# Recurrent state with an MLP behind it: one operand transposed once, kept in DRAM, and a gap between two preparation steps

## The chip, the cores and the metric

The kernel runs on one core of a Trainium2 chip. A core has a matrix engine (PE, whose weight loads are listed as PEld), a vector engine (DVE), a scalar engine (ACT), a general engine (POOL, also called GpSimd) and SyncE (SP), which here does nothing but issue DMAs. Each engine works through its own list of instructions in the order in which the program wrote them, and waits on semaphores for the others. DMAs of one core share 16 transfer engines. The metric is the device time of one execution in microseconds (us); the time of a kernel is the median of its runs.

## The reference

Six inputs r, k, v, w, a, b have the shape (4, 8, 768, 40): 4 batches, 8 heads, 768 tokens and 40 numbers per token. For each of the 32 heads a 40x40 state runs along the tokens; each token first reads the state, then changes it. The outputs of all heads of a token form a row of 320 numbers, which goes through two matrices with a piecewise quadratic gate between them.

```python
for t in range(S):
    y[:, :, t] = np.einsum('bhd,bhde->bhe', rt, state)
    Sa = np.einsum('bhde,bhe->bhd', state, at)
    state_decay = state * wt[:, :, None, :] - np.einsum('bhd,bhe->bhde', Sa, bt)
    state = state_decay + np.einsum('bhd,bhe->bhde', vt, kt)
...
x = np.ascontiguousarray(attn_out.transpose(0, 2, 1, 3)).reshape(B * S, H * D)
h = x @ w_in
g = np.where(pos, h, np.where(neg, 0.0, (h + beta) ** 2 / (4.0 * beta)))
return (g @ w_out).astype(np.float32)
```

w_in is 320 x 2048, w_out 2048 x 320, all in float32.

## The kernel before

**Chunks, halves and sets.** The 768 tokens are cut into 24 chunks of 32 tokens, and four chunks make a set of 128 tokens, of which there are six (numbered 0 to 5). Inside a chunk the recurrence is written as matrix products; only the state passes from chunk to chunk. Each chunk is worked on in two halves, `hb` 0 and 1, of 16 heads each. The heads of a half stand in two groups of partitions, 0 to 63 and 64 to 127 (`f` is 0 or 1).

**Three preparation steps, set by set.** They run ahead of the chunks that use them.

- *Token rows* (`prelude`, lines 232 to 278). In four parts of eight tokens: running products of w with two scans on DVE (line 221), then R, V and the scaled K, P, A and B. P is w's running product, A and B are a and b multiplied or divided by it. The results are gathered in the tile `arena` and stored by POOL to the DRAM buffer `scr` (line 275), which has one row of 240 numbers per head and token: R, V, K, P, A, B, 40 each. R and V are copied from DRAM to DRAM by `copy_rv` (line 129). Every part begins with POOL clearing two columns of `wz` (line 246) and ACT copying w into it (line 247).
- *Pair products* (`ab_set`, lines 292 to 324). For each of the set's four chunks, A and B of all 32 heads are loaded into the tile `tiab` (`load_rows`, line 290, four DMAs), transposed by DVE into `ea` (line 304) half by half, and multiplied on PE (line 313) to 32x32 products of each pair of tokens. ACT copies them to `pairs` (line 320). There is one `tiab`; the next chunk's load waits until the transposes have read it.
- *Inverse* (`invert`, lines 326 to 351). A triangular solve of 31 steps, each with two instructions on POOL (lines 343 and 349). `adopt` (line 357) takes the result over when the set's first chunk begins.

Sets 0 and 1 are prepared at the start by functions of their own: `early_products`, then `early_turn` (line 187 transposes A and B by PE, ACT copies them out in line 189 to `turned`), `early_ab` (line 203) and `early_store` (line 211). The tiles of `turned` are borrowed from the cg buffers and from `Y`; `init_cg` clears the cg buffers afterwards.

**A chunk.** For each half, `load_ti` (line 414) loads R, V, K, P and A of 16 heads into `tih`, with four DMAs, and `load_cg` loads V, K and B into one of three `cg` buffers, with four DMAs (lines 423 and 426). `turn` transposes on DVE: part 0 A into cg (line 442, two instructions), part 1 V and K into `ev`, part 2 R and P into `pr` (line 447). `scores` multiplies them on PE (line 457) and masks the products into cg (line 466). `chain` has four steps, each ending in a yield: lines 488 to 492, 498 to 509, 511 to 545, and 551 to 560.

**The MLP.** Per 64 tokens, `relayout` moves Y into X with nine DMAs (lines 574, 580, 584), and `moe` issues the first product (line 603), the gate (lines 611 to 613), a split into two floats (ACT line 619, POOL line 620) and the second product (line 632). Its matmuls are fed between the steps of the chunks by `fill`.

**What sets the order.** The order of each engine's list is written out by hand, at the end of the function: a chunk has four stages, each with one step of each half's chain, the turns, scores and loads of the next chunk, and a `fill`. `fill` calls `background` six times, which advances the three preparation steps. `WINDOWS` says for the sets 1 to 5 from when to when, in tenths of a chunk, a step is spread out; each step is a generator that yields weights (`ROWS_W`, `AB_W`, `INV_W`), and `background` advances it until the sum of its weights is the share of the window that has passed. A window of (0, 0) stands for the work done at the start. All loads of a chunk, all loads of the preparation, `copy_rv`, the relayout and the output go through the one list of SP, in this order of writing.

```python
WINDOWS = dict(
    rows=[(0, 0), (14, 36), (38, 62), (66, 102), (106, 142)],
    ab=[(0, 0), (36, 44), (62, 79), (102, 119), (142, 159)],
    inv=[(12, 38), (44, 78), (81, 118), (121, 158), (161, 198)],
)
```

Of the kernel before, what the change touches and what calls it, by code (L numbers as in the profile page):

```python
# [24 lines left out]


WINDOWS = dict(
    rows=[(0, 0), (14, 36), (38, 62), (66, 102), (106, 142)],
    ab=[(0, 0), (36, 44), (62, 79), (102, 119), (142, 159)],
    inv=[(12, 38), (44, 78), (81, 118), (121, 158), (161, 198)],  # L30
)

SHARE = (1.4, 0.6) * 2
SLOTS = len(SHARE)

ROWS_W = (2, 2, 4, 2, 6, 6, 4)
AB_W = (1, 4, 1, 4, 12, 15)
INV_W = 12

# [11 lines left out]
def rwkv_moe_kernel(ctx: ExitStack, tc: tile.TileContext, r, k, v, w, a, b, w_in, w_out, ident_d, mask_d, out):  # L51
# [28 lines left out]
    wz = const.tile([128, D, 10], F32, name="wz")  # L80
    dz = const.tile([128, D, 10], F32, name="dz")
    tiab = const.tile([128, 16, 80], F32, name="tiab")
    tih = [const.tile([128, 8, 200], F32, name=f"ti{i}") for i in range(2)]
    lw = const.tile([128, 2048 + 256], F32, name="lw")
    cgf = [const.tile([128, 16 * CW + 24], F32, name=f"cg{i}") for i in range(3)]
    cgs = [x[:, 0 : 16 * CW].rearrange("p (h x) -> p h x", x=CW) for x in cgf]
# [8 lines left out]
    work = ctx.enter_context(tc.tile_pool(name="work", bufs=1))  # L95
    scr = [dram.tile([NH * 128 + 1, RW], F32, name=f"scr{s}") for s in range(NS)]
    scr4 = [x[0 : NH * 128].rearrange("(b c t) x -> c b t x", c=4, t=L) for x in scr]
    pairs = const.tile([128, 32, 32], F32, name="pairs")
    tinv = const.tile([128, 4, 8, 32], F32, name="tinv")
    pairs_f = pairs.rearrange("p m i -> p (m i)")  # L100
    srcs = {n: x.rearrange("b h (c t) e -> (b h) c t e", t=L) for n, x in dict(k=k, w=w, a=a, b=b).items()}

    nc.gpsimd.memset(dz, 0.0)

    def zero(x, row=0):
        z = zero_c[row : row + x.shape[0]]
# [26 lines left out]
    def pad_scr(s):  # L133
# [2 lines left out]
    flat = lambda x: x.rearrange("p a e -> p (a e)")  # L136
    early_in = [
        [wides[0][:, 1280 * i : 1280 * i + 1280] for i in range(4)],
        [flat(tih[0])[:, 0:1280], flat(tih[1])[:, 0:1280], flat(tiab), Yraw[:, 0:1280]],
    ]  # L140
    early_in = [[x.rearrange("p (t e) -> p t e", e=D) for x in xs] for xs in early_in]
    early_out = [x.rearrange("p (t x) -> p t x", x=160) for x in (wides[1], wides[0])]
# [38 lines left out]
    def early_turn(s, j, part):  # L181

        for i in range(2):
# [4 lines left out]
            for f in range(2):  # L188
# [2 lines left out]
                    ps[0:D].rearrange("e t (p f c) -> e f p c t", f=2, c=4)[:, f],  # L191
                )

    def early_ab(s, half):

        ps = psum()
        for c in (2 * half, 2 * half + 1):
            for h in range(NH):
                p, f = h // 2, h % 2
                q, n = 2 * f + p % 2, 4 * p + c  # L200
                rows = slice(64 * f, 64 * f + D)
                at = 256 * (c % 2) + 32 * (p // 2)
                nc.tensor.matmul(
                    ps[32 * q : 32 * q + 32, at : at + 32],
                    lhsT=turned[s][0][rows, n, :], rhs=turned[s][1][rows, n, :], start=True, stop=True,
                )
        nc.scalar.copy(pairs_f[:, 512 * half : 512 * half + 512], ps)
# [17 lines left out]
    def prelude(s):  # L225
# [17 lines left out]
        yield 10  # L243
        for part in range(4):
            ts_ = slice(8 * part, 8 * part + 8)
            nc.gpsimd.memset(wz[:, :, 0::9], 0.0)
            nc.scalar.copy(rows_(wz)[:, 1:9], wl[1])
            yield ROWS_W[0]
            Pc = wl[0].rearrange("p (e t) -> p e t", t=10)
            if part == 0:  # L250
                nc.vector.memset(dz[:, :, 0], -1.0)
            scan(Pc, wz, dz)
            yield ROWS_W[1]
            if part < 3:
                nc.vector.tensor_copy(dz[:, :, 0], Pc[:, :, 8])
            nc.vector.reciprocal(dz[:, :, 9], Pc[:, :, 8])
            nc.scalar.copy(P, rows_(Pc)[:, 1:9])
            nc.gpsimd.tensor_mul(at, al, rows_(Pc)[:, 0:8])
            yield 1
            scan(wz, wz, dz, -1)  # L260
            rec = rows_(wz)[:, 2:10]
            for i in range(2):
                copy_rv(s, i, part)
            yield ROWS_W[2]
            bl = load("b", part)
            yield ROWS_W[3]
            nc.gpsimd.tensor_mul(kt, kl, rec)
            if part < 3:
                wl = load("w", part + 1)
            yield ROWS_W[4]  # L270
            if part < 3:
                al = load("a", part + 1)
            yield ROWS_W[5]
            nc.gpsimd.tensor_mul(bt, bl, rec)
            nc.gpsimd.dma_start(scr[s][0 : NH * 128, 80:240].rearrange("(p t) x -> p t x", t=L)[:, ts_, :], R)
            yield ROWS_W[6]
            if part < 3:
                kl = load("k", part + 1)
# [13 lines left out]
    def ab_set(s):  # L292

        if 9 in lending:
            reclaim(9)
            pad_rows(tiab, 48)
        load_rows(tiab, 4 * s, O_A, 80)
        yield AB_W[5]
        for c in range(4 * s, 4 * s + 4):
            tv = tiab.rearrange("p h (j x) -> p h j x", x=40)[:, :, :, 0:32]  # L300
            for half in range(2):
                ea = work.tile([128, 8, 2, 32], F32, tag="ea", name="ea")
                for i in range(2):
                    nc.vector.transpose(ea[:, 4 * i : 4 * i + 4], tv[:, 8 * half + 4 * i : 8 * half + 4 * i + 4])  # L304
                    yield AB_W[0]
                yield AB_W[1]
                ps = psum()[:, 0:128]
                for p in range(8):
                    for f in range(2):
                        rows = slice(64 * f, 64 * f + D)  # L310
                        q = 2 * f + p % 2
                        sl = p // 2
                        nc.tensor.matmul(  # L313
                            ps[32 * q : 32 * q + 32, 32 * sl : 32 * sl + 32],
                            lhsT=ea[rows, p, 0, :], rhs=ea[rows, p, 1, :], start=True, stop=True,
                        )
                assert s - 1 in turned_in
                at = 256 * (c % 4) + 128 * half
                yield AB_W[2]
                nc.scalar.copy(pairs_f[:, at : at + 128], ps)  # L320
                yield AB_W[3]
            if c < 4 * s + 3:
                load_rows(tiab, c + 1, O_A, 80)
                yield AB_W[4]
# [86 lines left out]
    def load_ti(c, hb):  # L411
        drain("rows", c // 4)
        tis[c, hb] = tih[hb]
        load_rows(tih[hb], c, 0, 200, 16 * hb, 16)

    def load_cg(c, hb):
        cg = cgs[(2 * c + hb) % 3]
        hsel = slice(16 * hb, 16 * hb + 16)
        drain("rows", c // 4)
        sc = scr4[c // 4][c % 4][hsel]  # L420
        for f in range(2):
            vr, ur = 64 * (1 - f), 64 * (1 - f) + 32
            nc.sync.dma_start(
# [11 lines left out]
    def turn(c, hb, part):  # L435
        u = 2 * c + hb
        cg, pr = cgs[u % 3], prs[u % 3]
        t5 = tis[c, hb].rearrange("p h (j x) -> p h j x", x=40)[:, :, :, 0:32]
        if part == 0:
            for f in range(2):  # L440
                rows = slice(64 * f, 64 * f + 64)
                nc.vector.transpose(cg[rows, f::2, C_X : C_X + 32], t5[rows, :, 4, :])
        elif part == 1:
            evs[u] = work.tile([128, 8, 2, 32], F32, tag="ev", name="ev")
            nc.vector.transpose(evs[u], t5[:, :, 1:3, :])
        else:
# [344 lines left out]
            early_turn(0, j, k)  # L791
    for half in range(2):
        early_ab(0, half)
    step_back("inv", 0)
    early_products(1)
    for k in range(2):
        init_cg(k, 0)
    for x in tih:
        pad_rows(x, 168)
    for k in range(2):  # L800
        init_cg(k, 1)
    early_store(0, 0)
# [9 lines left out]
    at = lambda n, f: todo.setdefault(n, []).append(f)  # L812

    def ahead(hb):
        for j in range(3):
            turn(0, hb, j)
        scores(0, hb)
        if NC > 1:
# [4 lines left out]
            at(2 + 4 * j + k, lambda j=j, k=k: early_turn(1, j, k))  # L823
    at(13, lambda: early_ab(1, 0))
    at(14, lambda: early_ab(1, 1))
    at(16, lambda: init_cg(2, 0))
    at(17, lambda: init_cg(2, 1))
    at(36, lambda: ahead(0))
# [58 lines left out]
    for c in range(NC + 1):  # L887
# [17 lines left out]
            load_ti(c + 1, 1)  # L905
        if nxt:
            load_cg(c + 1, 0)
            turn(c + 1, 0, 0)
        fill()
        for g, (t0, nt) in enumerate(groups):  # L910
            if t0 + nt == 32 * c:
# [16 lines left out]
        if nxt:  # L928
            scores(c + 1, 0)
            load_cg(c + 1, 1)  # L930
            turn(c + 1, 1, 0)
        fill()
    for _ in mgen:
        catch_up()
# [31 lines left out]
```

## Time and profile before

| | |
|---|---|
| median of 3 runs | 992.13 us (988.73 to 993.32) |
| the profiled execution | 995.83 us, of which 994.0 us from its first to its last instruction |
| mean granted clock of PE in the profiled execution | 0.829 |
| busy | PE 718.4 us, DVE 597.6, ACT 416.1, POOL 435.1 |
| DMA | 121.97 MB in 223161 packets |

The profile is one execution recorded by the chip. Its views are read as follows. The page gives busy times, the granted PE clock in slices, and the chain that ended last. A group row names line, engine, operation, output and inputs, count, then busy time and the mean of one, then the idle time of the engine just before. A row of the waits names who waited for whom, then the total in us, how many times, and the longest. A row of the timeline begins with start and duration in us, then engine, line and operation, and may end in the idle time before it and who ended that. A row of the windows has the stretch, then its length, then busy time and instruction count of PE, PEld, DVE, ACT and POOL, then PE's granted clock, the busy share of the transfer engines and GB/s. A row that belongs to one source line has the shortest, median and longest duration in ns, then the first and the last start. "SPq" marks SP's issuing of DMAs.

### The profile page before, as it was taken

How to read it: one execution, taken by the hardware profiler on the slowest of the kernel's cores; microseconds unless marked ns; L12 is line 12 of the kernel's file. 1: busy time of each engine (PE TensorE's matmuls, PEld its weight loads, DVE VectorE, ACT ScalarE, POOL GpSimd, SP SyncE). 2: the span in 40 equal slices, each digit the busy share in tenths (PEclk: the TensorE clock that was granted, in tenths of full speed). 3: DMA queues.
4: the chain of work that ended last, by engine and by line, in shares of the span. 5: the costliest groups of instructions: out<-in, count | busy, mean ns of one | idle time of the engine just before them, and what ended most of it. 6: DMA issues, size and time to landing. Idle time of an engine off the chain costs nothing.

```text
span 994.0 us, 34830 instructions
## 1 busy us (share of the span) xinstructions
PE 718.4 (72%) x14976; PEld 647.8 (65%) x14976; DVE 597.6 (60%) x1362; ACT 416.1 (42%) x896; POOL 435.1 (44%) x594
## 2 busy tenths in 40 slices
PE   4442413565776687688786588787799999999995
PEld 3231312454676576577676578676789888899894
DVE  5787777562646555477754486754477767677310
ACT  5543343231323433335433345433245555555552
POOL 3301234883224765435853345855225763222332
PEclk9565555576768788779988799988789999999998
DMA  9399966675557756657646666646535453543000
GB/s 295 68 188 267 228 132 136 165 154 106 90 107 168 142 103 125 115 129 165 143 97 121 116 142 154 141 92 125 104 67 104 85 120 69 127 84 72 17 32 14
DMA packets 223161, 121.97 MB, mean 123 GB/s; under 512 B 142824, under 2 KB 214696, under 8 KB 223008
## 3 DMA queue, kind: packets, MB, share of 16 engines
q1 hardware_dynamic: 219808, 108.61, 52.5%
q0 software_dynamic: 3200, 11.14, 3.6%
q8 instruction: 118, 1.93, 0.9%
q14 instruction: 35, 0.29, 0.1%
HBM read 90.54 MB, written 27.53 MB: 119 GB/s over the span
## 4 chain that ended last, share of the span: by engine, by line
PE 35%; DMA 17%; POOL 14%; DVE 11%; SPq 8%; ACT 7%; issue 7%; POOLq 0%; DVEq 0%; ACTq 0%
PE po L632 12%; PE ph L603 9%; POOL gl L620 5%; DMA scr<-arena 5%; PE p L525 4%; DMA tiab<-scr 4%; SPq L290 3%; PE p L514 3%; DMA ti<-scr 3%; POOL lw L343 3%; POOL lw L349 3%; ACT gh L619 2%; PE p L488 2%; PE p L554 2%; ACT cg L509 1%
## 5 line engine op out<-in xcount | busy, mean ns | idle before, releaser
L620 POOL TENSOR_TENSOR gl<-gt,gh 128x512 fp32r<-128x512 f32 x96 | 123.5, 1286 | 333.3 <-ACT gh L619 333.3
L603 PE MATMUL ph<-X,w 120*128 120x256 f32 x1536 | 223.9, 299 | 9.6 <-DMA X<-Y 4.9
L603 PEld LDWEIGHTS ph<-X,w 120*128 120x128 f32 x1536 | 201.6, 200 | 18.9 <-issue 11.3
L632 PE MATMUL po<-wide,gh 128*128 128x320 f32 x768 | 158.9, 330 | 30.8 <-ACT gh L619 30.8
L632 PEld LDWEIGHTS po<-wide,gh 128*128 128x128 f32 x768 | 127.9, 204 | 33.8 <-ACT gh L619 33.1
L613 DVE SCALAR_TENSOR_TENSOR gt<-gt,ph 128x512 f32<-128x512 f32 x96 | 65.8, 685 | 115.4 <-ACT gt L612 91.2
L632 PE MATMUL po<-wide,gl 128*128 128x320 f32 x384 | 100.1, 345 | 31.8 <-POOL gl L620 31.5
L532 DVE SCALAR_TENSOR_TENSOR cg<-p,pr 40x160 f32<-40x160 f32 x184 | 59.2, 322 | 82.7 <-PE p L525 80.7
L509 ACT ACTIVATE cg<-p 32x160 f32<-32x160 f32 x192 | 56.6, 295 | 106.0 <-PE p L498 78.7
L611 ACT ACTIVATE gt<-ph,half_c 128x512 f32<-128x512 f32 x96 | 66.0, 688 | 80.9 <-PE ph L603 80.8
L632 PEld LDWEIGHTS po<-wide,gl 128*128 128x128 f32 x384 | 68.3, 207 | 42.1 <-POOL gl L620 41.8
L349 POOL TENSOR_TENSOR lw<-lw 128x31 f32<-128x31 f32 (+15 forms) x155 | 90.2, 582 | 8.0
L466 DVE TENSOR_TENSOR cg<-p,mask 32x256 f32<-32x256 f32 x192 | 80.6, 420 | 14.5 <-PE p L457 11.2
L343 POOL TENSOR_TENSOR lw<-lw 128x31 f32<-128x31 f32 (+15 forms) x155 | 82.2, 531 | 8.5
L514 PE MATMUL p<-cg 128*40 128x40 f32 x1472 | 47.0, 231 | 43.4 <-ACT cg L509 43.4
L514 PEld LDWEIGHTS p<-cg 128*40 128x40 f32 x1472 | 40.6, 143 | 54.5 <-ACT cg L509 44.4
L519 ACT COPY ss<-p 40x320 f32<-40x320 f32 x92 | 38.6, 419 | 87.9 <-PE p L514 86.6
L525 PE MATMUL p<-cg 128*64 128x72 f32 (+1 forms) x1536 | 69.7, 253 | 0.2 <-issue 0.2
L505 DVE SCALAR_TENSOR_TENSOR cg<-p,mask 32x128 f32<-32x128 f32 x192 | 55.3, 288 | 16.0 <-ACT cg L509 9.1
L525 PEld LDWEIGHTS p<-cg 128*64 128x64 f32 x1536 | 64.1, 161 | 0.7 <-issue 0.5
L619 ACT CAST gh<-gt 128x512 fp32r<-128x512 f32 x96 | 59.7, 622 | 10.6 <-DVE gt L613 8.6
L313 PE MATMUL p<-ea 40*32 40x32 f32 x1024 | 19.3, 215 | 61.9 <-DVE ea L304 61.5
(108 smaller groups left out, 1083.8 us busy)
## 6 DMA issues: line engine op xcount, KB each, us to landing
ti<-scr SPq DMA_DIRECT2D x96, 200.0 KB
ti<-scr SPq DMA_DIRECT2D x96, 168.0 KB
scr<-arena POOLq DMA_DIRECT2D x16, 640.0 KB, 5.8
cg<-scr SPq DMA_DIRECT2D x96, 80.0 KB
X<-Y SPq DMA_DIRECT2D x36, 160.0 KB
scr<-wide SPq DMA_DIRECT2D x8, 640.0 KB
tiab<-scr SPq DMA_DIRECT2D x32, 160.0 KB
scr<-in_r_dram SPq DMA_DIRECT2D x24, 160.0 KB
```

Of the source, the lines that this page charges most:

```text
L343: eng.tensor_mul(t3, W3[:, 0:n, j : j + 1].broadcast_to([128, n, m]), L3[:, j + 1 :, j].unsqueeze(1).broadcast_to([128, n, m]),)
L349: eng.tensor_sub(W3[:, 0:n, j + 1 :], W3[:, 0:n, j + 1 :], t3)
L466: nc.vector.tensor_tensor(out=cg[q, f::2, C_X : C_X + 64][:, 4 * i : 4 * i + 4].rearrange("p h (j x) -> p h j x", x=32), in0=ps[quarter(f, ...
L509: nc.scalar.mul(cg[q, f + 2 * j :: 4, C_S : C_S + D], psv[j][quarter(f, j), :, 32:72], -1.0)
L514: nc.tensor.matmul(pst[er[h % 2], h // 2, :], lhsT=cg[:, h, C_S : C_S + D], rhs=cg[:, h, C_G : C_G + D], start=True, stop=True)
L525: nc.tensor.matmul(psv[h // 8][64 * f : 64 * f + 64, h // 2 % 4, 0:n3], lhsT=cgw[:, h * CW + C_G : h * CW + C_G + 64], rhs=cg[:, h, C_R : ...
L603: nc.tensor.matmul(phs[k % 2][:, n * j : n * j + n], lhsT=w1[:, wi, fs], rhs=Xs[g][:, xi, :], start=i == 0, stop=i == 7)
L611: nc.scalar.activation(gt, ph, AF.Relu, bias=half_c, scale=0.5)
L613: nc.vector.scalar_tensor_tensor(out=gt, in0=gt, scalar=1.0, in1=ph, op0=ALU.min, op1=ALU.max)
L619: nc.scalar.copy(gh, gt)
L620: nc.gpsimd.tensor_sub(gl, gt, gh.bitcast(F32))
L632: nc.tensor.matmul(pos[i], lhsT=x[:, ts_], rhs=w, start=at, stop=end)
```

## The change

A is no longer loaded with the token rows and transposed in every chunk. The step that makes the pair products transposes it anyway; now that transposed A is written to a new DRAM buffer `axt`, and `load_cg` loads it from there straight into its rows of cg. For this `ea` holds A and B in two separate blocks and has two buffers, each half of a chunk stores its A with two DMAs on SP, and ACT's copy of the products comes one yield earlier. For sets 0 and 1 the new `early_keep` writes A from `turned`, eight DMAs per set. `load_ti` loads 160 numbers per token in place of 200, the `tih` tiles shrink, and part 0 of `turn` is gone. `load_cg` gets two more DMAs. In the token rows, the clearing of `wz` moves from the start of a part to the end of the part before it (and once to the start of the kernel), and the last weight of a part goes from 4 to 8. The windows leave four or five tenths of a chunk between the end of the token rows and the beginning of the pair products.

```diff
-    rows=[(0, 0), (14, 36), (38, 62), (66, 102), (106, 142)],
-    ab=[(0, 0), (36, 44), (62, 79), (102, 119), (142, 159)],
-    inv=[(12, 38), (44, 78), (81, 118), (121, 158), (161, 198)],
+    rows=[(0, 0), (12, 33), (38, 58), (66, 98), (106, 138)],
+    ab=[(0, 0), (37, 46), (63, 79), (103, 119), (143, 159)],
+    inv=[(12, 36), (47, 78), (81, 118), (121, 158), (161, 198)],
...
-ROWS_W = (2, 2, 4, 2, 6, 6, 4)
+ROWS_W = (2, 2, 4, 2, 6, 6, 8)
...
-    tih = [const.tile([128, 8, 200], F32, name=f"ti{i}") for i in range(2)]
+    tih = [const.tile([128, 8, 160], F32, name=f"ti{i}") for i in range(2)]
...
+    axt = [dram.tile([4, 2, D, 16, L], F32, name=f"axt{s}") for s in range(NS)]
...
     nc.gpsimd.memset(dz, 0.0)
+    nc.gpsimd.memset(wz[:, :, 0::9], 0.0)
...
+    def early_keep(s, c):
+
+        for f in range(2):
+            nc.sync.dma_start(axt[s][c, f], turned[s][0][64 * f : 64 * f + D, c::4])
...
         for part in range(4):
             ts_ = slice(8 * part, 8 * part + 8)
-            nc.gpsimd.memset(wz[:, :, 0::9], 0.0)
             nc.scalar.copy(rows_(wz)[:, 1:9], wl[1])
...
             nc.gpsimd.dma_start(scr[s][0 : NH * 128, 80:240].rearrange("(p t) x -> p t x", t=L)[:, ts_, :], R)
+            nc.gpsimd.memset(wz[:, :, 0::9], 0.0)
             yield ROWS_W[6]
...
-                ea = work.tile([128, 8, 2, 32], F32, tag="ea", name="ea")
+                ea = work.tile([128, 2, 8, 32], F32, tag="ea", name="ea", bufs=2)
+                er = ea.rearrange("p j h t -> p h j t")
                 for i in range(2):
-                    nc.vector.transpose(ea[:, 4 * i : 4 * i + 4], tv[:, 8 * half + 4 * i : 8 * half + 4 * i + 4])
+                    nc.vector.transpose(er[:, 4 * i : 4 * i + 4], tv[:, 8 * half + 4 * i : 8 * half + 4 * i + 4])
...
-                            lhsT=ea[rows, p, 0, :], rhs=ea[rows, p, 1, :], start=True, stop=True,
+                            lhsT=ea[rows, 0, p, :], rhs=ea[rows, 1, p, :], start=True, stop=True,
                         )
                 assert s - 1 in turned_in
                 at = 256 * (c % 4) + 128 * half
+                nc.scalar.copy(pairs_f[:, at : at + 128], ps)
                 yield AB_W[2]
-                nc.scalar.copy(pairs_f[:, at : at + 128], ps)
+                for f in range(2):
+                    nc.sync.dma_start(axt[s][c % 4, f, :, 8 * half : 8 * half + 8], ea[64 * f : 64 * f + D, 0])
                 yield AB_W[3]
...
-        load_rows(tih[hb], c, 0, 200, 16 * hb, 16)
+        load_rows(tih[hb], c, 0, 160, 16 * hb, 16)
...
         sc = scr4[c // 4][c % 4][hsel]
+        drain("ab", c // 4)
+        for f in range(2):
+            nc.sync.dma_start(
+                cg[64 * f : 64 * f + D, f::2, C_X : C_X + 32], axt[c // 4][c % 4, f, :, 8 * hb : 8 * hb + 8]
+            )
...
-        if part == 0:
-            for f in range(2):
-                rows = slice(64 * f, 64 * f + 64)
-                nc.vector.transpose(cg[rows, f::2, C_X : C_X + 32], t5[rows, :, 4, :])
-        elif part == 1:
+        if part == 1:
...
     for half in range(2):
         early_ab(0, half)
+    for c in range(4):
+        early_keep(0, c)
...
-        pad_rows(x, 168)
+        pad_rows(x, 128)
...
-        for j in range(3):
+        for j in (1, 2):
             turn(0, hb, j)
...
     at(14, lambda: early_ab(1, 1))
+    at(15, lambda: [early_keep(1, c) for c in range(4)])
     at(16, lambda: init_cg(2, 0))
...
             load_cg(c + 1, 0)
-            turn(c + 1, 0, 0)
...
             load_cg(c + 1, 1)
-            turn(c + 1, 1, 0)
```

More of the change, by code (lines that the diff above doesn't have):

```diff
@@ L138, in rwkv_moe_kernel @@
         [wides[0][:, 1280 * i : 1280 * i + 1280] for i in range(4)],
-        [flat(tih[0])[:, 0:1280], flat(tih[1])[:, 0:1280], flat(tiab), Yraw[:, 0:1280]],
+        [flat(tih[0]), flat(tih[1]), flat(tiab), Yraw[:, 0:1280]],
     ]
```

## The prediction, made before the changed kernel ran

> **What bounds the kernel now.** I began with the page: busy shares, granted clock and the chain of waits.
>
> ```profile
> span 994.0 us, 34830 instructions
> ...
> PEclk9565555576768788779988799988789999999998
> ...
> PE po L632 12%; PE ph L603 9%; POOL gl L620 5%; DMA scr<-arena 5%; PE p L525 4%; DMA tiab<-scr 4%; SPq L290 3%; PE p L514 3%; DMA ti<-scr 3%; POOL lw L343 3%; POOL lw L349 3%; ACT gh L619 2%; PE p L488 2%; PE p L554 2%; ACT cg L509 1%
> ```
>
> PE's granted clock, in tenths over 40 slices, is 9 in the last quarter and 5 to 9 before it. The chain holds two transfers of the preparation, scr<-arena (5%) and tiab<-scr (4%), and SP itself. To see where they bite I cut the span at the copies of line 492, two per chunk, and asked for windows of two chunks each.
>
> ```profile
> L492 ACT COPY x<-p x48: 398/401/402, 72.5 to 926.6; 128x288 f32<-128x288 f32 x48
> ...
> core 0: us, PE busy (x) PEld busy (x) DVE busy (x) ACT busy (x) POOL busy (x), PEclk, DMA share, GB/s
> ...
> 352.90:439.90 87.00, 63.78 (x1377) 57.89 (x1377) 47.17 (x114) 31.35 (x70) 42.60 (x59) 0.80 0.62 124
> 439.90:502.00 62.10, 52.76 (x1121) 47.90 (x1122) 45.28 (x98) 29.42 (x63) 38.77 (x53) 0.95 0.61 134
> 502.00:587.40 85.40, 61.57 (x1377) 55.60 (x1378) 47.16 (x115) 31.31 (x71) 39.56 (x55) 0.86 0.64 125
> 587.40:651.40 64.00, 54.88 (x1121) 49.66 (x1122) 45.29 (x98) 29.32 (x62) 38.77 (x53) 0.92 0.59 133
> 651.40:732.30 80.90, 66.65 (x1377) 60.70 (x1378) 41.19 (x104) 28.75 (x66) 33.10 (x48) 0.81 0.51 99
> 732.30:785.50 53.20, 50.14 (x1121) 45.83 (x1122) 39.28 (x91) 26.66 (x59) 27.97 (x42) 1.00 0.49 98
> ```
>
> The six rows are chunks 6-7, 8-9, 10-11, 12-13, 14-15 and 16-17. Pair products (ab) run in the first, third and fifth, token rows alone in the second and fourth, neither in the sixth. The two kinds of preparation do not cost alike: a pair of chunks with pair products takes 87.0, 85.4, 80.9 us, one with rows alone 62.1 and 64.0. The excess over the rows pair behind it (for the last, over 64.0) is 24.9, 21.4 and 16.9, together 63 us. PE has 256 matmuls more in them beside 1121, but what differs most is its idle time, 23.2, 23.8 and 14.3 us against 9.3 and 9.1, and its clock, 0.80 to 0.86 against 0.92 and 0.95.
>
> The waits of SP, and SP's own timeline in chunks 9 to 11, name the first cause:
>
> ```profile
> SPq L290 <- DMA scr<-arena: 69.7, 4, 19.1
> SPq L290 <- DVE ea L304: 41.6, 8, 8.2
> ...
> 492.91 0.45 SPq L426 DMA_DIRECT2D cg<-scr  x1
> 512.01 1.90 SPq L290 DMA_DIRECT2D tiab<-scr  x4
> ...
> 529.74 2.02 SPq L290 DMA_DIRECT2D tiab<-scr  x4
> ...
> 546.35 4.31 SPq L290 DMA_DIRECT2D tiab<-scr  x4
> ```
>
> Once per set (four times, 69.7 us) SP stands at the first tiab load of line 290 until the last store of the token rows has landed, here from 493 to 512. Behind it stand the chunk's ti and cg loads, the nine relayout DMAs and then the second tiab load, which is why that one comes only at 529.74. DVE then waits for it, and PE for DVE:
>
> ```profile
> 535.96 0.77 DVE L304 STREAM_TRANSPOSE ea<-tiab 128x256 f32<-128x256 f32 x2 [5.42 <-DMA tiab<-scr]
> ...
> 536.55 0.67 PE L313 MATMUL p<-ea 40*32 40x32 f32 x32 [5.36 <-DVE ea L304]
> ```
>
> So up to 730 us the bound is a queue order (SP, then DVE, then PE), and from there PE.
>
> **The change, part by part.**
>
> **The gap between rows and pair products.** The last store is emitted at 33, 58, 98 and 138 tenths of a chunk and the load at 37, 63, 103 and 143: four or five tenths, 13 to 16 us of a 32 us chunk. The SP waits were 69.7/4 = 17.4 us, and rows also end three to four tenths earlier, so the wait should all but go. What it cost is PE's idle time behind it; PE's waits in the four windows 223-248, 344-390, 493-541 and 640-686 are:
>
> ```profile
> PE p L313 <- DVE ea L304: 11.2, 1, 11.2
> ...
> PE p L313 <- DVE ea L304: 5.7, 1, 5.7
> ...
> PE p L313 <- DVE ea L304: 5.4, 1, 5.4
> PE ph L603 <- issue: 2.2, 1, 2.2
> ...
> PE p L313 <- DVE ea L304: 3.3, 1, 3.3
> ```
>
> That is 27.8 us. The waits of these windows on POOL and ACT stay, as they come from other work. A stall also costs clock. A stretch that begins in a stall of chunk 11, and the one after it:
>
> ```profile
> 551.80:565.50 13.70, 7.34 (x175) 6.90 (x176) 5.66 (x15) 1.96 (x6) 3.49 (x7) 0.50 0.71 120
> 565.50:580.00 14.50, 12.06 (x332) 10.67 (x332) 9.06 (x23) 6.92 (x16) 5.55 (x8) 1.00 0.45 110
> ```
>
> 175 matmuls in 13.7 us against 332 in 14.5: at the second row's rate they take 7.6 us, so 6 us were lost, some of it the idle time itself. I take 4 us per stall, 16 for four. What is late next is the first load itself: its 1.90 us of issue and 4.2 us to land (531.76 to 535.96 for the second load above), 6.1 us, against 15 of the set's 139 weights, 5.4 us of a window of 16 tenths or 50 us; with SP's other work in between, 2 us each remain, 8 in all. Term: -(27.8 + 16 - 8) = **-36**; bounds -10 (the wait only moves) and -63 - (11.2+4) = -78 (all excess of the three pairs goes, and the stall of the first set).
>
> **Pair products store A.** Each half set gets two more DMAs on SP, 40 partitions wide. The nearest rows are the relayout's 40-partition DMAs, beside the 32-partition ones of cg and the tiab pieces:
>
> ```profile
> L580 SPq DMA_DIRECT2D X<-Y x48: 706/707/1441, 192.7 to 946.3; - x48
> ...
> L423 SPq DMA_DIRECT2D cg<-scr x96: 302/395/1511, 42.5 to 903.8; - x96
> ...
> L290 SPq DMA_DIRECT2D tiab<-scr x64: 302/486/2711, 240.1 to 708.8; - x64
> ```
>
> Two at 0.71 with gaps make 1.5 us. They wait for the transposes, as the next tiab load does, and stand ahead of that load: loads two to four of four sets, 12 loads, come 1.5 us later, 18 us at most. SP waited for the transposes 8 times (41.6 us, above), and where it did the delay is whole:
>
> ```profile
> DVE ea L304 <- DMA tiab<-scr: 57.9, 12, 9.5
> ```
>
> 12 of 16 loads keep DVE waiting, so little hides it. I take 8 x 1.5 = **+12**; bounds 0 and 12 x 5.4 (both stores at 2.71) = +65. The second ea buffer and the earlier ACT copy of pairs (one weight, 50/139 = 0.36 us) count as nothing.
>
> **A loaded into its rows.** 96 transposes of line 442 leave DVE:
>
> ```profile
> L442 DVE STREAM_TRANSPOSE cg<-ti 64x256 f32<-64x256 f32 x96 | 42.2, 440 | 2.7
> ```
>
> 42.2 us, but the page's chain has no L442 among its lines, and in chunks 16-17 DVE is busy 39 of 53 us beside PE's 50. I take a tenth, **-4**; bounds 0 and -20. In exchange each half chunk's cg load has two more DMAs, 1.5 us of SP, 48 times, and the ti loads shrink by a fifth. The new data are needed sooner than the old cg data, by scores. The shortest time from cg issue to the mask behind scores:
>
> ```profile
> 665.94 0.40 SPq L423 DMA_DIRECT2D cg<-scr  x1
> ...
> 677.51 1.72 DVE L466 TENSOR_TENSOR cg<-p,mask 32x256 f32<-32x256 f32 x4
> ```
>
> 11.6 us, the matmuls of scores among it, against 1.5 us of issue and the 4.2 us to land from above, so 5.9 us to spare. That hides it: 0. If the cover went, the price were the 1.5 us each, +72. Reuse of the buffer adds no wait: the old loads already wait for the same matmuls.
>
> **A kept at the start.** Sixteen DMAs of 640 pieces of 128 bytes. Those of set 0 fall where SP is free:
>
> ```profile
> ACT ti L107 <- DVE arena L173: 7.2, 1, 7.2
> ...
> 19.04 0.69 SPq L211 DMA_DIRECT2D scr<-wide  x1
> 40.53 1.82 SPq L290 DMA_DIRECT2D ti<-scr  x4
> ```
>
> Eight of 0.7 to 1.5 us end before 33, and ACT, which then clears the buffer they read, waits 7.2 us for DVE next: 0. Those of set 1 come near 62 us, where the transfer engines are 0.93 busy:
>
> ```profile
> 50.00:75.00 25.00, 10.40 (x442) 8.22 (x439) 20.62 (x49) 11.87 (x25) 0.20 (x1) 0.64 0.93 190
> ...
> q1 hardware_dynamic: 219808, 108.61, 52.5%
> ```
>
> The queue's row gives 0.525 x 16 x 994 us / 219808 = 38 ns for a mean packet of 494 bytes. 5120 packets are 12 us of sixteen engines at that, 3 us if time goes by bytes. I take the middle, since the row is a mean over both small and large, **+6**; bounds 0 and +15. The wait it adds, ACT's clearing of the third cg buffer, holds the conversion of weights behind it for the same time; that is in the bound.
>
> The Trainium skill, "DMA: Bandwidth & Descriptors", section "Why a DMA increments its semaphore by 16 and not by 1", says that a transfer is spread over the largest number of engines up to 16 that divides its outer dimensions, ten for 40 partitions. By that rule the same packets would take 1.6 times as long, and the sum would come out some 4 us later, 970. No row here shows engines apart; the issue time (0.71 us for 40 partitions, 0.40 for 32) agrees that the two kinds differ.
>
> **Rows.** The clearing of wz goes behind the store, so DVE's scan no longer stands behind GpSimd's backlog, and eight weights instead of four stand between store and next part:
>
> ```profile
> DVE ld_w L221 <- POOL wz L246: 24.7, 7, 5.9
> ...
> ACT arena L257 <- DMA scr<-arena: 29.6, 6, 5.6
> ```
>
> The windows are shorter too (36 to 32 tenths, 24 to 20), so from store to ACT's copy it is 12/130 x 20 = 1.85 tenths where it was 8/114 x 24 = 1.68: ACT's wait hardly moves. DVE's mostly goes, but is partly covered by that same ACT. I take **-4**; bounds +10 (denser rows) and -25.
>
> **Sum:** -36 + 12 - 4 + 6 - 4 = -26. The profiled execution took 995.8 us, 1.8 beyond its span, and would take 969.8; it stands 3.7 above the median of the runs, 992.1. On the median's scale: **966 us**.
>
> **Rivals.** (1) **Slower: the stores hold SP.** Place: the two stores per half set, ahead of each tiab load. If a load comes later by a whole wait of today's kind, 41.6/8 = 5.2 us, 12 loads cost 62 in place of 12 and the time is 1016. It decides from (36+4+4-6)/12 = 3.2 us per load, 1.6 per store; 0.71 and 1.44 speak against it, the 2.71 of one tiab piece for it. (2) **The wait moves.** GpSimd issues the last store late because its own queue is late, DVE still waits for tiab, and the gap brings 10, not 36: 992. For it: 12 of 16 loads wait today, most not at the arena store. Against it: the gap is as long as the stalls. (3) **All of the excess goes**, since every later load comes on time once SP has no backlog: -78 in place of -36 and +12, 992 - 80 = 912 at the extreme; with half of the further gain, about 938. Against it: the load at 546 is late with SP long free of the stall.
>
> **How the numbers follow.** Forecast (945 to 984) 0.58; (1) 0.20, with its lighter forms from 997 up; (2) 0.12; (3) 0.10. Half a percent, 5 us, is about what a measurement of this kernel can tell from no change. Faster by more: 0.67; within: 0.12; slower by more: 0.21. The range reaches from 935 to 1005: it leaves out the extreme of (3) and the upper half of (1). The likeliest case alone has 945 to 984.
>
> **What would show it.** The SP wait for scr<-arena near 0 and PE's four waits gone; windows of chunks 10-11 and 14-15 at 68 to 75 us, with a clock of 0.9; DVE's wait for tiab still there, 40 us or more; the new stores at 0.7 us; chunk 0 no more than 6 us later. Wrong it would be if SP's wait for ea grew beyond 80 us, if scores waited for the new loads, or if chunk 4 came over 15 us later.

## The result and the profile after

The changed kernel took 942.9 us (median of 4 runs, 942.6 to 950.4); the kernel before, beside it, 991.5 us. The ratio is 0.953, with a 95% interval of 0.948 to 0.958: 48.6 us faster, where 26 were forecast. One run of the experiments below, of E4 (954.7 us, its others 940.0 to 944.4), was in the chip's slower state and is left out.

The page of the changed kernel, its span and PE's granted clock in 40 slices (mean 0.850), then the windows of the same chunk pairs as before (6-7 to 16-17), cut at the same ACT copies, which are line 503 now:

```profile
span 940.4 us, 34992 instructions
...
PEclk9565555667868888799898799898999999999998
```

```profile
335.30:411.70 76.40, 60.89 (x1377) 54.29 (x1378) 44.07 (x105) 31.40 (x70) 43.57 (x61) 0.89 0.66 135
411.70:472.90 61.20, 53.65 (x1121) 48.72 (x1122) 40.73 (x90) 29.49 (x63) 38.60 (x55) 0.94 0.64 144
472.90:548.90 76.00, 61.98 (x1377) 55.67 (x1377) 44.41 (x106) 31.60 (x70) 38.41 (x53) 0.87 0.69 140
548.90:610.00 61.10, 53.16 (x1121) 48.38 (x1122) 41.16 (x90) 29.26 (x62) 38.88 (x55) 0.94 0.62 139
610.00:678.60 68.60, 59.88 (x1377) 54.12 (x1378) 37.56 (x97) 28.80 (x67) 31.19 (x46) 0.90 0.56 112
678.60:731.70 53.10, 50.02 (x1121) 45.70 (x1121) 35.68 (x83) 26.58 (x58) 27.95 (x42) 1.00 0.43 92
```

The three pairs of chunks that contain pair products (first, third, fifth row) lost 10.6, 9.4 and 12.3 us; those with rows alone lost 0.9 and 2.9; from chunk 16 on nothing changed. The waits of SP and of the engines:

```profile
SPq L330 <- DVE ea L312: 34.8, 12, 5.9
...
SPq L297 <- DMA scr<-arena: 6.5, 1, 6.5
```

```profile
PE p L321 <- DVE ea L312: 30.8, 22, 4.8
...
DVE ea L312 <- DMA tiab<-scr: 15.6, 5, 6.6
...
ACT cg L109 <- DMA ti<-scr: 11.1, 1, 11.1
```

SP's wait for the arena store fell from 69.7 us to 6.5, and DVE's wait for tiab with it, from 57.9 us in 12 pieces to 15.6 in 5. The last row is new: ACT, clearing the third cg buffer, waits 11.1 us for the stores of A that read it (the profile names another DMA, the one it saw last; in E4 below, where these stores read another tile, the wait is gone). The rows of the new DMAs, from the views of their lines (shortest, median, longest in ns):

```profile
L330 SPq DMA_DIRECT2D axt<-ea x64: 272/327/1119, 241.2 to 673.6; - x64
...
L433 SPq DMA_DIRECT2D cg<-axt x96: 286/341/1457, 42.1 to 851.0; - x96
...
L199 SPq DMA_DIRECT2D axt<-cg x16: 747/832/2719, 18.2 to 69.8; - x16
```

Issues of 0.33 us in the pair products, not 0.71. Only the stores at the start (line 199) take as long to issue as was assumed.

### The profile page after: what moved, and what is told of

Its sections match the earlier page's. It is cut to its first block, busy times and chain, and to the rows that moved or that the text cites. A ratio compares the mean times of both kernels' runs of the same rounds, so it can differ in the third digit from the quotient of the medians.

```text
span 940.4 us, 34992 instructions
## 1 busy us (share of the span) xinstructions
PE 707.0 (75%) x14976; PEld 637.1 (68%) x14976; DVE 556.1 (59%) x1266; ACT 416.3 (44%) x896; POOL 433.4 (46%) x595
## 5 line engine op out<-in xcount | busy, mean ns | idle before, releaser
L614 PEld LDWEIGHTS ph<-X,w 120*128 120x128 f32 x1536 | 199.1, 198 | 10.7 <-issue 2.8
L643 PE MATMUL po<-wide,gh 128*128 128x320 f32 x768 | 156.8, 327 | 11.2 <-ACT gh L630 11.2
L643 PEld LDWEIGHTS po<-wide,gh 128*128 128x128 f32 x768 | 126.7, 202 | 13.4 <-ACT gh L630 12.6
L643 PE MATMUL po<-wide,gl 128*128 128x320 f32 x384 | 99.4, 342 | 38.5 <-POOL gl L631 38.2
L543 DVE SCALAR_TENSOR_TENSOR cg<-p,pr 40x160 f32<-40x160 f32 x184 | 59.2, 322 | 90.1 <-PE p L536 87.9
L643 PEld LDWEIGHTS po<-wide,gl 128*128 128x128 f32 x384 | 67.3, 205 | 49.9 <-POOL gl L631 49.8
L359 POOL TENSOR_TENSOR lw<-lw 128x31 f32<-128x31 f32 (+15 forms) x155 | 89.1, 575 | 9.1
L353 POOL TENSOR_TENSOR lw<-lw 128x31 f32<-128x31 f32 (+15 forms) x155 | 80.5, 519 | 8.6
L525 PE MATMUL p<-cg 128*40 128x40 f32 x1472 | 45.8, 227 | 44.7 <-ACT cg L520 44.6
L530 ACT COPY ss<-p 40x320 f32<-40x320 f32 x92 | 38.5, 419 | 78.5 <-PE p L525 76.9
L565 PE MATMUL p<-pr,ss 40*40 40x32 f32 x1472 | 41.4, 210 | 33.6 <-DVE pr L458 28.8
L536 PE MATMUL p<-cg 128*64 128x72 f32 (+1 forms) x1536 | 66.4, 246 | 0.0
L565 PEld LDWEIGHTS p<-pr,ss 40*40 40x40 f32 x1472 | 36.2, 130 | 43.1 <-issue 21.8
L623 ACT ACTIVATE gt<-gt 128x512 f32<-128x512 f32 x96 | 60.6, 631 | 3.0
```

Of the source, the lines that this page charges most:

```text
L353: eng.tensor_mul(t3, W3[:, 0:n, j : j + 1].broadcast_to([128, n, m]), L3[:, j + 1 :, j].unsqueeze(1).broadcast_to([128, n, m]),)
L359: eng.tensor_sub(W3[:, 0:n, j + 1 :], W3[:, 0:n, j + 1 :], t3)
L525: nc.tensor.matmul(pst[er[h % 2], h // 2, :], lhsT=cg[:, h, C_S : C_S + D], rhs=cg[:, h, C_G : C_G + D], start=True, stop=True)
L536: nc.tensor.matmul(psv[h // 8][64 * f : 64 * f + 64, h // 2 % 4, 0:n3], lhsT=cgw[:, h * CW + C_G : h * CW + C_G + 64], rhs=cg[:, h, C_R : ...
L565: nc.tensor.matmul(psv[er[f], p, :], lhsT=ss[er[f], p, :], rhs=pn[er[f], p, 0, 8:40], start=True, stop=True)
L614: nc.tensor.matmul(phs[k % 2][:, n * j : n * j + n], lhsT=w1[:, wi, fs], rhs=Xs[g][:, xi, :], start=i == 0, stop=i == 7)
```

## The experiments

Every ratio is to the kernel before, run beside it on the same chip. E1 to E4 ran on one chip, E5 to E8 on a second and E9 to E12 on a third, so across these groups, and against the changed kernel's own result, the ratios are compared and not the microseconds. The profiles are cut into stretches by the starts of the x0 copies (line 492 before, two per chunk). Differences of stretches are between single executions; the profiled one of the kernel before (995.8 us) is 4 us above its median there and 8 above the one beside E1 to E3 (987.9), so what is gained against it looks that much larger.

**1 to 3: the schedule without A, A without the schedule, the windows alone.** The first theory was that the schedule brings nearly all.

E1, the kernel before with the new schedule:

```diff
-    rows=[(0, 0), (14, 36), (38, 62), (66, 102), (106, 142)],
-    ab=[(0, 0), (36, 44), (62, 79), (102, 119), (142, 159)],
-    inv=[(12, 38), (44, 78), (81, 118), (121, 158), (161, 198)],
+    rows=[(0, 0), (12, 33), (38, 58), (66, 98), (106, 138)],
+    ab=[(0, 0), (37, 46), (63, 79), (103, 119), (143, 159)],
+    inv=[(12, 36), (47, 78), (81, 118), (121, 158), (161, 198)],
...
-ROWS_W = (2, 2, 4, 2, 6, 6, 4)
+ROWS_W = (2, 2, 4, 2, 6, 6, 8)
...
+    nc.gpsimd.memset(wz[:, :, 0::9], 0.0)
...
-            nc.gpsimd.memset(wz[:, :, 0::9], 0.0)
             nc.scalar.copy(rows_(wz)[:, 1:9], wl[1])
...
             nc.gpsimd.dma_start(scr[s][0 : NH * 128, 80:240].rearrange("(p t) x -> p t x", t=L)[:, ts_, :], R)
+            nc.gpsimd.memset(wz[:, :, 0::9], 0.0)
```

> The kernel before with the new windows, the new last weight of a part and the moved clearing of wz; A is loaded and transposed as before. Theory S (the schedule brings nearly all of the gain; A kept in DRAM costs about 5 us at the start and brings little): 943 to 952 us, as the start is 5 us earlier than in the changed kernel and the chunks are alike. Rival D (A's path brings about half, by DVE and smaller loads): 962 to 970 us.

Measured: 929.0 us, ratio 0.940 (0.937 to 0.943). That is below the bands of both theories, and faster than the changed kernel: the schedule brings more than the whole gain.

E2 takes the same lines back in the changed kernel, so that only A's path is left.

> The changed kernel with the old windows, the old last weight and the old place of the clearing: only A's new path. Theory S: 985 to 997 us, SP's wait for the arena store still 60 us or more. Rival D: 965 to 972 us.

Measured: 997.9 us, ratio 1.008 (1.004 to 1.012); SP's wait for the arena store is 65.2 us. A's path alone makes the kernel 0.8% slower.

E3 is E1 with the three lines of `WINDOWS` only.

> The kernel before with the new windows alone. If the gap alone does it: within 5 us of e1_gap. If the moved clearing and the longer end of a part carry a share: 8 us or more above e1_gap, with DVE's wait for the clearing of wz still 20 us or more.

Measured: 944.7 us, ratio 0.956 (0.952 to 0.960). The second case holds, but DVE's wait for the clearing is 13.8 us, not 20. SP's wait for the arena store is down to 7.6 us, once. PE's wait for the transposes, before and in E3, and DVE's wait for tiab in E3:

```profile
PE p L313 <- DVE ea L304: 61.5, 17, 11.2
```

```profile
PE p L313 <- DVE ea L304: 31.5, 24, 3.0
...
DVE ea L304 <- DMA tiab<-scr: 19.8, 5, 6.0
```

Where the time went, in us of the profiled executions:

| stretch | before | E3 windows | E1 schedule | changed |
|---|---|---|---|---|
| start to chunk 3 | 204.9 | 210.9 | 209.0 | 210.1 |
| chunk 3 | 56.5 | 36.3 | 37.3 | 36.4 |
| chunk 4 | 50.6 | 45.8 | 47.6 | 50.3 |
| chunk 5 | 40.9 | 37.8 | 37.8 | 38.5 |
| chunks 6-7 | 87.0 | 75.5 | 74.1 | 76.4 |
| chunks 8-9 (rows) | 62.1 | 66.4 | 59.2 | 61.2 |
| chunks 10-11 | 85.4 | 74.9 | 73.7 | 76.0 |
| chunks 12-13 (rows) | 64.0 | 66.4 | 61.1 | 61.1 |
| chunks 14-15 | 80.9 | 67.3 | 65.8 | 68.6 |
| from chunk 16 | 261.7 | 261.7 | 262.1 | 261.8 |

The windows take 63.7 us out of the chunks that hold pair products or stand beside them (3 to 7, 10, 11, 14, 15) and give 12.7 back: 6.0 before chunk 3 and 6.7 in the pairs with rows alone. The rest of the schedule (E1) takes 12.5 back out of those pairs. What it mends is seen in chunk 9, here of the kernel before, E3 and E1 in this order (one row of windows each):

```profile
469.20:502.00 32.80, 27.18 (x561) 24.80 (x562) 21.10 (x48) 14.26 (x31) 23.41 (x32) 0.90 0.53 117
```

```profile
433.30:472.70 39.40, 29.18 (x561) 26.67 (x562) 20.47 (x49) 14.25 (x31) 24.75 (x34) 0.83 0.55 115
```

```profile
432.80:465.00 32.20, 26.45 (x561) 24.08 (x562) 20.54 (x48) 14.40 (x30) 22.86 (x32) 0.95 0.65 140
```

and in the waits of the three over the whole span, in the same order:

```profile
PE po L632 <- ACT gh L619: 30.8, 11, 6.7
...
ACT wz L247 <- POOL arena L274: 17.7, 6, 5.5
```

```profile
ACT arena L257 <- DMA scr<-arena: 35.2, 9, 6.6
...
ACT wz L247 <- POOL arena L274: 27.0, 9, 5.9
PE po L632 <- ACT gh L619: 26.8, 8, 6.9
```

```profile
ACT arena L257 <- DMA scr<-arena: 19.1, 4, 6.0
...
ACT wz L247 <- POOL arena L274: 13.0, 4, 4.2
PE po L633 <- ACT gh L620: 12.7, 8, 6.0
```

ACT's two copies at the beginning of a part wait for the end of the part before: 29.6 + 17.7 = 47.3 us before, 62.2 with the shorter windows, 32.1 with the schedule whole. PE's wait for the MLP's gh copy, which stands behind them in ACT's list, follows only in the last.

**9 and 10: which half of that.** E9 is the kernel before with the moved clearing and the last weight 8, in the old windows. E10 is E1 with the last weight at 4.

```diff
-ROWS_W = (2, 2, 4, 2, 6, 6, 8)
+ROWS_W = (2, 2, 4, 2, 6, 6, 4)
```

> The kernel before with the moved clearing of wz and the last weight of a part at 8, old windows. If that term is worth by itself what it is with the new windows (e3_windows to e1_gap, 0.956 to 0.940): 0.982 to 0.986 of before, DVE's wait for the clearing gone. If it only repairs what the denser rows cost: 0.993 to 1.000.

Measured: 975.2 us, ratio 0.989 (0.985 to 0.993), between the two cases: in the old windows the term is worth about 1%. Its waits show that it takes ACT's waits of the rows and PE's for gh down and leaves those of SP for the arena store, of DVE for tiab and of PE for the transposes where they were:

```profile
SPq L291 <- DMA scr<-arena: 65.2, 4, 17.6
```

```profile
PE p L314 <- DVE ea L305: 59.6, 18, 10.5
DVE ea L305 <- DMA tiab<-scr: 57.7, 11, 8.8
...
ACT arena L257 <- DMA scr<-arena: 23.0, 5, 5.4
...
PE po L633 <- ACT gh L620: 13.1, 8, 5.1
```

> The new windows and the moved clearing of wz, the last weight of a part at 4 as before. If the clearing carries the term: 0.938 to 0.943 of before, like e1_gap. If the longer end of a part carries it: 0.951 to 0.957, like e3_windows.

Measured: 946.2 us, ratio 0.962 (0.957 to 0.966): no better than the windows alone. The waits are those of E3 too:

```profile
ACT arena L257 <- DMA scr<-arena: 34.4, 8, 7.1
...
ACT wz L247 <- POOL arena L274: 30.9, 9, 7.5
PE po L633 <- ACT gh L620: 29.4, 9, 7.8
```

ACT's two waits come to 65.3 us, and to 32.1 in E1, which differs only in the last weight. So the clearing's new place alone brings nothing, and the longer end of a part, which keeps ACT's next copies away from the store, is needed. The longer end with the clearing at its old place was not run.

**5 to 8: what A's path costs.** The changed kernel is 1.3% of the time before behind E1 (0.953 against 0.940, intervals apart).

E5 leaves the stores behind the pair products out:

```diff
-                for f in range(2):
-                    nc.sync.dma_start(axt[s][c % 4, f, :, 8 * half : 8 * half + 8], ea[64 * f : 64 * f + D, 0])
...
-                cg[64 * f : 64 * f + D, f::2, C_X : C_X + 32], axt[c // 4][c % 4, f, :, 8 * hb : 8 * hb + 8]
+                cg[64 * f : 64 * f + D, f::2, C_X : C_X + 32], axt[min(c // 4, 1)][c % 4, f, :, 8 * hb : 8 * hb + 8]
```

> The changed kernel without the 64 stores of A behind the pair products; the sets 2 to 5 load the A of set 1, so their results are not the reference's. The gap alone ran at 0.940 of before, the change at 0.953, about 13 us apart. Theory Q (the stores stand in SP's queue ahead of the tiab loads and cost 10 to 13 us): 0.940 to 0.944 of before, 929 to 934 us. Rival L (the loads of A into cg cost it): 0.951 to 0.954.

Measured: 936.6 us, ratio 0.947 (0.943 to 0.951). (In the changed kernel no row of SP's waits has the loads of A waiting for these stores, so E5 frees them of no wait that shows.)

E6 leaves out the loop with the load of line 433.

> The changed kernel without the 96 loads of A into cg: A counts as zero in the scores, so the results are not the reference's; stores kept. Theory Q: 0.950 to 0.954 of before. Rival L: 0.940 to 0.944.

Measured: 935.9 us, ratio 0.946 (0.942 to 0.950). Neither theory holds alone: stores and loads take about 6 and 7 us, but both intervals overlap that of the changed kernel at one end, so that each size is uncertain by some 6 us. Against E7 below, which has both and ran on the same chip (941.4 us), they are 4.8 and 5.5 us. The places tell more than the medians. Start to chunk 4, then chunk 4 (pair products of set 2) of the changed kernel, E5 and E6:

```profile
76.50:246.50 170.00, 77.08 (x1889) 69.23 (x1889) 106.07 (x232) 65.54 (x145) 82.04 (x119) 0.63 0.76 177
246.50:296.80 50.30, 36.84 (x753) 33.17 (x754) 30.25 (x65) 18.72 (x42) 16.05 (x18) 0.73 0.69 157
```

```profile
76.00:248.10 172.10, 77.95 (x1889) 70.08 (x1890) 105.47 (x233) 65.59 (x146) 82.18 (x119) 0.64 0.76 175
248.10:295.20 47.10, 35.73 (x753) 31.91 (x754) 30.29 (x65) 18.79 (x42) 16.11 (x18) 0.75 0.68 153
```

```profile
74.90:242.10 167.20, 78.38 (x1889) 70.37 (x1890) 106.67 (x238) 65.78 (x147) 81.91 (x119) 0.62 0.75 176
242.10:292.10 50.00, 37.05 (x753) 33.31 (x753) 30.16 (x65) 18.70 (x42) 16.04 (x18) 0.73 0.66 154
```

Without the stores chunk 4 is 3.2 us shorter and the start is not; without the loads chunk 4 begins 4.4 us earlier and is no shorter. In all the stretches from chunk 4 on with pair products in them (4, 5, 6-7, 10-11 and 14-15) the changed kernel takes 309.8 us and E6 307.0; E4 and E7, which have the same stores, take 307.4 and 304.5; without the stores it is 300.4 (E5) and 299.0 (E1). So the stores cost where they are issued, in the pair products. The loads seem to cost mostly before chunk 4, but the margin is small: without them it begins only 2.6 us before the earliest of the kernels that have them (E7, 244.7).

E7 moves the stores of a chunk's second half behind the next tiab load:

```diff
+                def keep(c=c, half=half, ea=ea):
+                    for f in range(2):
+                        nc.sync.dma_start(axt[s][c % 4, f, :, 8 * half : 8 * half + 8], ea[64 * f : 64 * f + D, 0])
+                if half == 0:
+                    keep()
                 yield AB_W[3]
             if c < 4 * s + 3:
                 load_rows(tiab, c + 1, O_A, 80)
+            keep()
+            if c < 4 * s + 3:
                 yield AB_W[4]
```

> The changed kernel with the two stores of a chunk's second half issued behind the next tiab load in place of ahead of it. If it is their place ahead of the load that costs: most of 13 us comes back for three of eight half sets' loads, 0.943 to 0.948 of before. If it is the wait for DVE or the transfers, or the first half's stores: 0.951 to 0.955.

Measured: 941.4 us, ratio 0.951 (0.947 to 0.955), at the edge of the second band, with an interval that reaches into the first, and not to be told from the changed kernel. Whether the place of the second half's stores costs anything stays open.

E8 gives DVE its 96 transposes back:

```diff
-        if part == 1:
+        if part == 0:
+            for f in range(2):
+                rows = slice(64 * f, 64 * f + 64)
+                nc.vector.transpose(pr[rows, :, 1, 8:40], t5[rows, :, 3, :])
+        elif part == 1:
```

with the three calls of part 0 as before.

> The changed kernel with the 96 transposes back on DVE, at their old places and of the old size (they write P ahead of its own transposes, so nothing else changes). If DVE's relief of 42 us brings the tenth that the prediction took: 4 us slower, 0.956 to 0.958 of before. If it brings nothing: 0.952 to 0.954. If it is what pays for the stores: 10 us or more slower, 0.963 and up.

Measured: 950.9 us, ratio 0.960 (0.956 to 0.965): 7 us slower than the changed kernel, with intervals that overlap (9.5 us against E7 on the same chip), and between the first case and the third. By the medians the relief of DVE is worth a sixth to a quarter of its 42 us, and A's DMAs eat it.

**4: the wait at the start.** E4 exchanges the two tiles of set 1's turned A and B:

```diff
-        [x[:, 0:2048].rearrange("p (n t) -> p n t", t=L) for x in xs] for xs in ((cgf[0], cgf[1]), (cgf[2], Yraw))
+        [x[:, 0:2048].rearrange("p (n t) -> p n t", t=L) for x in xs] for xs in ((cgf[0], cgf[1]), (Yraw, cgf[2]))
```

> The changed kernel with the two tiles of the turned A and B of set 1 exchanged: A stands in Y's tile, B in the third cg buffer, so ACT's clearing of that buffer no longer waits for the stores of A. If that wait (11.1 us) makes the first chunk late: its first copy comes 4 us earlier (72.5 in place of 76.5) and the time is 937 to 940. If SP's queue or the transfers make the start late: the first copy moves, later chunks do not, and the time is 942 to 944.

Measured: 940.4 us, ratio 0.952 (0.949 to 0.956), between the two cases and not to be told from the changed kernel. ACT's rows of E4 and chunk 0 of the changed kernel and of E4 (timeline, then windows):

```profile
62.27 2.13 ACT L109 COPY cg<-zero_c 128x2328 f32<-128x2328 f32 x1
...
70.74 0.40 ACT L503 COPY x<-p 128x288 f32<-128x288 f32 x1 [5.38 <-PE p L499]
```

```profile
76.50:118.80 42.30, 13.58 (x352) 12.02 (x352) 27.41 (x58) 18.00 (x41) 7.82 (x10) 0.57 1.00 242
```

```profile
70.70:119.40 48.70, 13.95 (x352) 12.31 (x352) 31.98 (x75) 17.92 (x41) 7.85 (x10) 0.54 0.99 231
```

The wait is gone and the first copy comes 5.8 us earlier, but chunk 0 then takes 6.4 us longer at the same full transfer engines (1.00 and 0.99): chunk 1 begins where it did (119.4 and 118.8). The wait was found, and by the places it cost nothing; why chunk 0 stretches instead was not tried.

**11 and 12: two tries to go on from E1.** In E1, PE waits 30 us at one place in chunk 1.

```diff
-    rows=[(0, 0), (12, 33), (38, 58), (66, 98), (106, 138)],
+    rows=[(0, 0), (14, 33), (38, 58), (66, 98), (106, 138)],
```

> e1_gap with the first window of token rows beginning at 14 tenths as before in place of 12, so that the two steps that take staging buffers back from the weights do not begin at once. In e1_gap PE waits 30 us at one place in chunk 1 and chunk 2 begins 4 us later than before. If that is the cause: chunk 2 begins at 172 and the time is 0.934 to 0.938 of before. If GpSimd's work for set 2 sets the pace up to chunk 3: 0.939 to 0.945.

Measured: 934.5 us, ratio 0.949 (0.945 to 0.953): outside both cases and about 1% slower than E1, with intervals apart. Chunks 1 and 2 of E1, then of E11 (windows):

```profile
115.60:176.10 60.50, 15.36 (x450) 13.71 (x450) 44.25 (x95) 23.63 (x52) 24.96 (x39) 0.56 0.69 162
...
176.10:209.00 32.90, 19.51 (x478) 17.84 (x478) 20.59 (x47) 9.47 (x22) 30.42 (x44) 0.66 0.79 185
```

```profile
115.70:170.80 55.10, 16.06 (x448) 14.39 (x448) 40.79 (x87) 22.15 (x50) 20.52 (x32) 0.55 0.66 154
170.80:213.20 42.40, 22.41 (x480) 19.94 (x480) 26.76 (x57) 11.15 (x24) 38.03 (x52) 0.63 0.78 174
```

Chunk 1 loses its 5.4 us, as expected, and chunk 2 gains 9.5: POOL's work has moved, from 25.0 to 20.5 us in chunk 1 and from 30.4 to 38.0 in chunk 2, which it fills to nine tenths in both kernels. The early start of the rows pays for itself there.

```diff
-AB_W = (1, 4, 1, 4, 12, 15)
+AB_W = (1, 8, 1, 2, 10, 14)
```

> e1_gap with the pair products' matmuls four weights further behind their transposes (AB_W 1, 8, 1, 2, 10, 14 in place of 1, 4, 1, 4, 12, 15). PE still waits 28.9 us for the transposes in 23 pieces of 1 to 3 us. If their nearness in the order is the cause: the wait falls below 15 us and the time to 0.925 to 0.935 of before. If DVE is late by more than the distance: no change, 0.938 to 0.943.

Measured: 926.2 us, ratio 0.942 (0.937 to 0.946): within E1's interval, as the second case had it. PE's wait for the transposes fell only from 28.9 to 25.9 us, while DVE's for tiab rose from 18.8 to 30.3:

```profile
DVE ea L305 <- DMA tiab<-scr: 30.3, 7, 7.1
...
PE p L314 <- DVE ea L305: 25.9, 19, 4.5
```

The best version found is the schedule without A's path, E1 or E12; the runs do not tell these two apart.

## Why the prediction was right, and where it missed

The direction and the place were right, and the time lies in the range from 935 to 1005: time was lost behind SP's wait for the arena store, and windows with a gap took it out. The size was about half. At 942.9 us the kernel lies below the likeliest case (945 to 984), near the 938 us that rival 3, with a chance of 0.10, gives with half of its gain.

The cause rests on the kernels side by side. Where SP's wait stays at 65 to 70 us (before, E2, E9), PE waits 59.6 to 70.9 us for the transposes, in pieces of up to 11.2 us; in the changed kernel and the others with the new windows SP waits at most 9.0 us and PE 25.9 to 32.5, in pieces of at most 5.3. But the windows change several things at once: the gap, the earlier end of the rows, and the times of the first two inverses. No run took SP's wait away and left the rest as it was, so the gap's own share is argued, not shown. Step by step:

**The gap, -36.** Measured with the windows alone: 0.956, some -43 us, and that is net of 12.7 us that the denser rows cost (the table). Gross that is some 56 (43 and 12.7), or 63.7 in the spans; the far bound was 78. The step that failed is the price of the wait: "What it cost is PE's idle time behind it", taken from one stall per set (27.8 us, 2.2 of them a row of line 603 that waits for nothing shown), with "the waits of these windows on POOL and ACT stay". In the stretches that lost the 63.7 us, PE's waits, added up over the views of their windows, fell from 111.2 us before to 65.0 in E3. Those for the transposes fell by 30.0, near the forecast, though 10.8 us of a new wait, for DVE's cg, stand against it. Those on ACT and POOL did not stay: gh from 23.4 to 11.3, gl from 13.7 to 9.6. Waits without a visible cause fell from 12.6 to 1.8. PE's busy time, with PE's clock at 0.78 to 0.92 in place of 0.73 to 0.86, fell by 12.9 us, near the 16 taken for the clock. Why the waits on ACT fell with the gap stays open.

"What is late next" was too dark as well: the later loads of a set were to stay late, and DVE's wait for tiab at 40 us or more. It fell from 57.9 us in 12 pieces to 19.8 in 5 (E3) and 15.6 in 5 (changed kernel), while in E9, where SP still waits 65.2 us, it stayed at 57.7. For the set in chunks 10 and 11 the four tiab loads are issued over 54.0 us before (512.0 to 566.0) and over 44.4 us in E3 (478.3 to 522.7): behind the long wait the queue did not catch up. This is the part of rival 3 that came true; most of the excess of 63 us did go.

**Rows, -4.** Mis-sized: -15.3 us in the spans from E3 to E1. The working looked at set 3 alone, where the distance from store to copy hardly changes, and at DVE's wait for the clearing. (The weights of a set's token rows add up to 10 + 4 x 27 = 118 before and 10 + 4 x 31 = 134 after, not 114 and 130; the distances are 1.63 and 1.79 tenths.) What counts is ACT's wait at the part's beginning, and the distance that the new windows would have had with the old weight: 8/118 x 20 = 1.36 tenths. E10 shows that the clearing's new place alone does nothing measurable there.

**A's path, +12, -4, 0 and +6: +14 together.** Measured from E1 to the changed kernel: +13. That the sums agree is luck, as the shares differ. Stores: about +6; the row taken for their issue was the wrong neighbour (0.71 us of the relayout; they took 0.33). DVE's relief: -7 instead of -4. Loads: +7 instead of 0; the cover was read in the chunks, and most of the loads' cost seems to lie before chunk 4, where the transfer engines are fullest (1.00 in chunk 0). Stores at the start: +6 was taken; the first chunk did come 4 us late, but in the table chunk 4 begins at 246.3 in E1 and 246.5 in the changed kernel, and E4 shows that the delay is absorbed in chunk 0. By place, then, A's path as a whole costs nothing before chunk 4, and 10.8 of the 12.7 us between the spans lie in the stretches with pair products, where the stores are. The shares 6 + 7 - 7 leave 7 of the 13 us over; each is uncertain by some 6 us, and what of the rest is theirs stays open.

**The other signs.** The pairs 10-11 and 14-15 took 76.0 and 68.6 us (68 to 75 was said) at a clock of 0.87 and 0.90, chunk 0 came 4 us later, and chunk 4 began earlier than before. The new stores' 0.33 us and DVE's 15.6 us were not what was said. None of the signs of being wrong appeared: SP's wait for ea stayed under 80 us, and no row has scores waiting for the new loads.

**Rival 1** (the stores hold SP) did not decide: SP's wait for ea at the stores is 34.8 us in 12 pieces, under today's 41.6, and a pair of issues takes 0.7 us, not 3.2. **Rival 2** fell with the waits: SP waits for the arena store in one set only (6.5 us once). That A's part of the change gains nothing was not among the rivals; only its sum of +14 said so.

The rule of the Trainium skill on the number of engines ("DMA: Bandwidth & Descriptors", "Why a DMA increments its semaphore by 16 and not by 1") gave 970 by a longer stay of the 40-partition transfers. No run here shows engines apart; but what the prediction read as agreement, a longer issue for 40 partitions, does not hold: lines 330 and 433 issue 40 partitions in 0.33 and 0.34 us.

## What to carry to other kernels

When one queue serves everything, price a wait in it by the whole stretch that runs late behind it, later loads of the same step and waits on other engines among them, and not by the one stall that its first victim shows. A change that comes in parts should be priced in parts: here a good schedule carried a data path that costs about 1% (0.8% in the old windows, 1.3% in the new), and only the kernel with the one and without the other shows it. Time saved on an engine that does not bound the stretch (42 us of DVE) is worth a fraction, and the DMAs that replace it can cost more than that.

## What the runs showed of the hardware that was not expected

Many more packets, at equal bytes, did not take more transfer time in sum. The queue's row of the changed kernel:

```profile
DMA packets 268442, 121.99 MB, mean 130 GB/s; under 512 B 185544, under 2 KB 259976, under 8 KB 268288
...
q1 hardware_dynamic: 265088, 108.62, 53.4%
```

45280 packets more than before on that queue, for the same 108.6 MB, took 0.534 x 940.4 = 502 us of each engine where it was 0.525 x 994.0 = 522. The mean packet took 30 ns against 38. Small packets are cheaper than the mean, not free: E6, with 31680 packets fewer, took 477 us of each engine, 25 less, or 12.5 ns per packet. In the changed kernel's trace the 41088 packets of 128 bytes have a mean of 16 ns; at that the prediction's 5120 take 5 us, not the 12 by the mean of all, and the +6 taken as the middle was near. And issue time does not follow the number of partitions alone: the relayout's 40-partition DMAs took 0.71 us of SP, the new ones 0.33 (line 330) and 0.34 (line 433). What makes the difference was not tried.
